# Third half of a fused attention and gated FFN: its q and k transposed by transfers instead of TensorE

## The chip, the cores and the metric

The kernel runs on one core of a Trainium2 chip. The metric is the device time of one execution in microseconds (us): the median of three runs is 237.72 us (236.86 to 237.77). The profiled execution took 237.94 us, of which the profile's span covers 236.1 us, at the full TensorE clock.

## The reference

Windowed attention with a linear distance bias, followed by a gated feed-forward layer over the same tokens (4 batches of 768 tokens, 8 heads of 64, feed-forward width 1536):

```python
scores = scale * q @ k.T                      # per batch and head, 768 x 768
keep   = (pos_k < 8) | ((rel >= 0) & (rel < 96))
scores = where(keep, scores - slope[h] * dist, -1e9)
a      = softmax(scores)
x      = (a @ v) -> [3072, 512]
out    = (relu(x @ w_gate) * (x @ w_val)) @ w_out
```

## The kernel before, in words

**Halves.** The 3072 tokens are cut into eight "halves" of 384, two to a batch, numbered 0 to 7. A half first goes through attention and then, as a chunk of 384 rows, through the feed-forward layer. The instruction order of every engine is written out by hand: `weave` takes a list of feed-forward pieces and drops other pieces at given fractions of it. `attention_pieces(s)` is the attention of half s, so TensorE does feed-forward products of earlier halves while it does the attention of the next.

**Operands of the scores.** TensorE needs q and k with the head dimension on the partitions, that is, transposed, and in bf16. `load_qk(s)` brings q and k of a half as float32 into `qs` and `ks`, which have one buffer each. Three routes lead on from there:

- Halves 0 and 1 use TensorE transposes with a layout of their own (`qTb`).
- Half 2, the third one, is cast by GpSimd into space of the result buffer `obuf` (`cast`, L263), eight casts in all, then transposed by TensorE against `ident` (`piece_t`, L299, into PSUM tiles of the pool `qk_ps`). VectorE moves the keys from PSUM into `kT[1]`, three copies for each pair of heads (`piece_copy_k`, L278 to L280), and ScalarE moves the queries into `qT2[0]` (L982). These are the four `T2_piece`s, placed at 0.55 to 0.95 of a weave of feed-forward products.
- Halves 3 to 7 use `early_pieces(s)`: GpSimd casts k and q into `kc` and `qc` (L367), transposing DMA transfers on the SP queue write `kN` and `qT2` (`piece_x`, L372, three for k and three for q), and GpSimd puts the keys in their order in `kT` (`piece_order`, L278 to L284).

**Values.** `load_v_half(s)` starts the loads of v on GpSimd's DMA queue. For an even half that is `load_v_globals` (L141, the first eight keys of the batch, which all queries see) and then four key tiles (L154); for batch 1 (half 2) three more tiles follow at once with `load_v_half(3)`. `spread_v_globals` (L146) copies the eight global rows into the six other key tiles by small DMA copies on the SP queue. The products of probabilities and values (L431) of half 2 need the first four key tiles and the first three of these copies.

**Weights.** `load_w_group(i)` loads 512 columns of `w_gate` and `w_val` each, cast to bf16 by the DMA; `wo_sb` is `w_out` as fp16. All are issued from GpSimd, so their data travel in the software DMA queue, in the order of issue, together with v and (for half 2 only) q and k. VectorE forms sums of blocks of `wo_sb` (L597) in the second weave, the first of them at 51.1 us.

**The order around the change.** On GpSimd: weight groups 1 and 2, q and k of half 2, `wo_sb`, some clearing of buffers, the eight casts, the loads of v. On the SP queue: nothing between the first loads of half 0 and the copies of global rows. On TensorE: the weave of feed-forward products of chunks 0 and 1 (L745), then from 48.3 us the scores of half 2 (L512), woven with the third weight group.

Of the kernel before, what the change touches and what calls it, by code (L numbers as in the profile page):

```python
# [16 lines left out]
def kernel(  # L17
# [12 lines left out]
    nc = tc.nc  # L30

    B, H, S, D = q.shape
# [6 lines left out]
    HP = H // 2  # L39
# [15 lines left out]
    for half in range(2):  # L55
# [35 lines left out]
    qT2 = [qTb[1].rearrange("d p e t -> d (p e t)")[:, i * HP * QH : (i + 1) * HP * QH].rearrange(  # L91
        "d (p t) -> d p t", p=HP) for i in range(2)]
# [20 lines left out]
    def load_qk(s, h0, h1, eng=nc.sync):  # L113
        b, half = divmod(s, 2)
        if s not in qs_of:
            qs_of[s] = stage.tile([128, H, NN * D], FP32, name="qs")
            ks_of[s] = stage.tile([128, H, NN * D], FP32, name="ks")
        for src, dst in ((k, ks_of[s]), (q, qs_of[s])):
            eng.dma_start(
                out=dst[:, h0:h1, :],  # L120
                in_=src[b, h0:h1, half * QH : (half + 1) * QH, :].rearrange(
                    "h (p n) d -> p h (n d)", n=NN))
# [17 lines left out]
    def load_v_globals(b):  # L140
        nc.gpsimd.dma_start(out=v_dst(b, 0, NG, 0),  # L141
                            in_=v[b, :, 0:NG, :].rearrange("h p d -> p h d"))

    def spread_v_globals(b, j0=1, j1=NT):
        for j in range(j0, j1):
            nc.sync.dma_start(out=v_dst(b, 0, NG, j), in_=v_dst(b, 0, NG, 0))  # L146
# [5 lines left out]
    def load_v(b, j, r0=0, r1=KT):  # L152
        n = min(r1, S - KT * j) - r0
        nc.gpsimd.dma_start(  # L154
            out=v_dst(b, NG + r0, NG + r0 + n, j),
            in_=v[b, :, KT * j + r0 : KT * j + r0 + n, :].rearrange("h p d -> p h d"))

    def fill_ones(eng, i, j):
        eng.memset(vbuf[i][:, j, :].bitcast(mybir.dt.uint32).rearrange(
            "p (h z) -> p h z", z=D // 2)[:, 0 : 2 * H + 1 : 2, :], 0x3F803F80)  # L160

    def load_v_half(s):
        b, half = divmod(s, 2)
        if half == 0:
            load_v_globals(b)
            spread_v_globals(b)
        for j in range(4) if half == 0 else range(4, NT):
            load_v(b, j)

    def load_w(dst, src, f0, f1):  # L170
        nc.gpsimd.dma_start(out=dst, in_=src[:, f0:f1].rearrange("(c p) f -> p c f", p=128))  # L171

    def load_w_group(i):
        load_w(wg[i], moe_w_gate, i * GW * 128, (i + 1) * GW * 128)
        load_w(wv[i], moe_w_val, i * GW * 128, (i + 1) * GW * 128)
# [67 lines left out]
    def setup_mask(h):  # L243
        nc.scalar.activation(m_all[:, h], dd, AF.Exp, bias=0.0, scale=-slopes[h])
# [6 lines left out]
    QKB, FFB, AVB = (qk_psum, "qk_ps"), (ff_psum, "ff_ps"), (av_psum, "av_ps")  # L251
# [6 lines left out]
    def piece_cast(s, p, i, eng):  # L258
        if (s, p) not in cast_of:
            cast_of[s, p] = oflat[:, 384 * p : 384 * (p + 1)].bitcast(BF16).rearrange(  # L260
                "t (i n e d) -> t i n e d", i=2, n=NN, e=2)
        src = (qs_of[s], ks_of[s])[i]
        (eng.copy if eng is nc.scalar else eng.tensor_copy)(  # L263
            cast_of[s, p][:, i].rearrange("t n e d -> t e n d"),
            src[:, 2 * p : 2 * p + 2, :].rearrange("t e (n d) -> t e n d", n=NN))

    def put_keys(copy, copy_small, kt, src, half):

        tk = src.rearrange("d (n p) -> d p n", n=NN)

        def put(j0, j1, p0, r0, r1):
            o = kt[:, j0:j1, r0:r1].rearrange("d j (p n) -> d j p n", n=NN)
            np_ = (r1 - r0) // NN
            i_ = tk[:, p0 : p0 + (j1 - j0) * np_, :].rearrange("d (j p) n -> d j p n", j=j1 - j0)
            return o, i_

        if half == 0:
            copy(*put(0, 3, 0, NG, 128))  # L278
            copy_small(*put(3, 4, 120, NG, NG + 24))
            copy_small(kt[:, :, 0:NG], kt[:, 0:1, NG : 2 * NG].to_broadcast([128, NT, NG]))  # L280
        else:
            copy(*put(4, 6, 32, NG, 128))
            copy_small(*put(3, 4, 0, NG + 24, 128))
            copy_small(*put(6, 7, 112, NG, NG + 48))  # L284

    tp_of = {}

    def piece_t(s, p, pool=av_psum, name="av_ps", apart=False):
        for i in (1, 0):
            if i == 1 or apart:  # L290
                tp = pool.tile([128, 512], FP32, name=name)
                tp = tp[:, 0:QH].bitcast(BF16).rearrange("d (i t) -> d i t", i=2)
            tp_of[s, p, i] = tp[:, i, :]
            for n in range(NN):
                for e in range(2 if s == 1 else 1):
                    r = slice(64 * e, 64 * e + 64) if s == 1 else slice(0, 128)
                    src = (qk16[s, i][:, 2 * p + e, n * D : (n + 1) * D] if s == 1
                           else cast_of[s, p][:, i, n])
                    nc.tensor.matmul(tp[r, i, n * 128 : (n + 1) * 128],  # L299
                                     lhsT=src, rhs=ident, is_transpose=True,  # L300
                                     start=((i == 1 or apart) and n == 0),
                                     stop=((i == 0 or apart) and n == NN - 1))

    def piece_copy_k(s, p):
        b, half = divmod(s, 2)
        put_keys(nc.vector.tensor_copy, nc.vector.tensor_copy, kT[b % 2][p], tp_of[s, p, 1], half)
# [59 lines left out]
    def piece_cast2(s, p, dst, src):  # L366
        nc.gpsimd.tensor_copy(  # L367
            dst[s % 2].rearrange("t n (h d) -> t h n d", d=D)[:, 2 * p : 2 * p + 2],
            src[s][:, 2 * p : 2 * p + 2, :].rearrange("t e (n d) -> t e n d", n=NN))

    def piece_x(dst, src, n):
        nc.sync.dma_start_transpose(out=dst[:, :, n * 128 : (n + 1) * 128], in_=src[:, n])  # L372

    def piece_order(s, p):
        b, half = divmod(s, 2)
        put_keys(nc.gpsimd.tensor_copy, nc.gpsimd.tensor_copy, kT[b % 2][p], kNb[s % 2][:, p], half)

    def early_pieces(s):
        out = [(0.0, lambda p=p: piece_cast2(s, p, kc, ks_of)) for p in range(HP)]
        out += [(0.0, lambda n=n: piece_x(kNb[s % 2], kc[s % 2], n)) for n in range(NN)]  # L380
        out += [(0.0, lambda p=p: piece_cast2(s, p, qc, qs_of)) for p in range(HP)]
        out += [(0.0, lambda n=n: piece_x(qT2[s % 2], qc[s % 2], n)) for n in range(NN)]
        out += [(0.0, lambda p=p: piece_order(s, p)) for p in range(HP)]
        return out
# [420 lines left out]
    def spread(items, first, last):  # L805

        n = len(items)
        return [(first + (i + 0.5) / n * (last - first), f) for i, (_, f) in enumerate(items)]

    def weave(f_items, *placed):  # L810
        total = sum(t for t, _ in f_items)
        a_items = sorted((x for p in placed for x in p), key=lambda x: x[0])
        done, ai = 0.0, 0
        for t, f in f_items:
            f()
            done += t
            while ai < len(a_items) and a_items[ai][0] * total <= done:
                a_items[ai][1]()
                ai += 1
        for _, f in a_items[ai:]:  # L820
            f()

    def cast(s, p, ek, eq):
        piece_cast(s, p, 1, ek)
        piece_cast(s, p, 0, eq)

    V, P, A = nc.vector, nc.gpsimd, nc.scalar
# [90 lines left out]
    piece_biased(1, 0)  # L918
    load_v(0, 3, 24)
    load_w_group(1)  # L920
    load_w_group(2)
    load_qk(2, 0, H, nc.gpsimd)
    load_w(wo_sb, moe_w_out, 0, DM)
    for f in gate[0:3]:
        f(0, LAST)
# [46 lines left out]
    nc.gpsimd.memset(vbuf[1][:, NT - 1, :].bitcast(mybir.dt.uint32), 0)  # L972
    for j in range(NT):
        fill_ones(nc.gpsimd, 1, j)
    for p in range(HP):
        cast(2, p, P, P)
    load_v_half(2)

    def T2_piece(p):
        piece_t(2, p, *QKB, apart=True)  # L980
        piece_copy_k(2, p)
        nc.scalar.copy(qT2[0][:, p], tp_of[2, p, 0])  # L982

    T2 = [(0.0, lambda p=p: T2_piece(p)) for p in range(HP)]
    weave(f1_1[G[0]] + f1_0[G[1]][4:] + f1_1[G[1]],
          [(0.05 + 0.06 * j, lambda j=j: fill_ones(nc.vector, 0, j)) for j in range(NT)],
          [(0.1 + 0.2 * i, lambda h=h: setup_mask(h)) for i, h in enumerate((0, 1, 6, 7))],
          [(0.6, lambda: load_qk(3, 0, H)), (0.6, lambda: load_v_half(3))],
          spread(T2, 0.55, 0.95))
    sums_wo = [(0.0, f) for i in (0, 3) for f in weight_sums(i, i + 3)]  # L990
    weave(f1_0[G[2]] + f1_1[G[2]] + f2_0 + f2_1,
          spread(attention_pieces(2), 0.02, 0.86), spread(early_pieces(3), 0.1, 0.76),
# [47 lines left out]
```

The softmax here doesn't subtract the row's maximum and nothing guards it: scores larger than these inputs give would overflow.

## Time and profile before

| what | value |
|---|---|
| median of three runs | 237.72 us |
| span of the profile | 236.1 us |
| TensorE busy | 228.7 us, 97% |
| VectorE busy | 186.9 us, 79% |
| ScalarE busy | 146.2 us, 62% |
| GpSimd busy | 89.0 us, 38% |
| mean DMA rate | 129 GB/s; in the four slices of 5.9 us from 23.6 to 47.2 us: 206, 262, 282, 171 |
| first load of weight group 1 to last landing of `wo_sb` | issued at 19.57 us, landed at 47.1 us |

Busy time of an engine is the union of its instructions. A DMA has two times: when the engine has issued it, and when it has landed; the DMA view gives the median from the one to the other. The DMA engines are sixteen and are shared by all queues: `q0` is the software queue fed by GpSimd, `q1` the hardware queue fed by SP. Their "share of 16 engines" counts the time of each packet from its start to its end; since packets overlap within an engine, a queue that keeps all engines full shows more than 100%.

### The profile page before, as it was taken

What the parts mean: (1) busy time and instruction counts of PE and PEld (TensorE: products, weight loads), DVE (VectorE), ACT (ScalarE), POOL (GpSimd) and SP (SyncE); (2) the same over time, 40 slices, a digit from 0 to 9 for tenths busy, and PEclk for the clock granted to TensorE, in tenths of its full rate; (3) what the DMA queues carried; (4) which work ended last, traced back from release to release, by engine and by line L of the source; (5) the groups of instructions that cost most, each with busy time, mean ns of one, the idle gap of its engine ahead of it and who ended that gap; (6) DMA issues with size and microseconds to landing.
All of it is one profiled execution on the core that took longest, in us unless ns stands there. A gap on an engine that the chain in (4) does not pass through costs nothing.

```text
span 236.1 us, 5512 instructions
## 1 busy us (share of the span) xinstructions
PE 228.7 (97%) x2021; PEld 157.7 (67%) x2021; DVE 186.9 (79%) x466; ACT 146.2 (62%) x321; POOL 89.0 (38%) x191
## 2 busy tenths in 40 slices
PE   7898999999999999999999999999999999999994
PEld 3674766656678666856688566856688566865683
DVE  6876867879988779886999779876899779863784
ACT  7988865667624887467842787557742687624310
POOL 8997913933483066406580066405340000000000
PEclk9999999999999999999999999999999999999999
DMA  5999999998459856856397764846412200020005
GB/s 167 203 168 183 206 262 282 171 118 267 72 155 170 250 149 106 52 176 204 90 81 119 236 175 90 53 143 214 93 44 89 92 0 3 0 92 0 1 3 178
DMA packets 71419, 30.43 MB, mean 129 GB/s; under 512 B 47744, under 2 KB 70784, under 8 KB 71392
## 3 DMA queue, kind: packets, MB, share of 16 engines
q0 software_dynamic: 34896, 10.27, 38.7%
q1 hardware_dynamic: 36496, 19.82, 29.7%
q8 instruction: 16, 0.26, 0.5%
q14 instruction: 11, 0.09, 0.1%
HBM read 28.38 MB, written 6.29 MB: 147 GB/s over the span
## 4 chain that ended last, share of the span: by engine, by line
PE 83%; DVE 5%; POOL 4%; DMA 4%; ACT 2%; issue 1%; POOLq 0%; DVEq 0%
PE ff_ps L745 49%; PE ff_ps L631 19%; PE av_ps L431 6%; DMA kc<-in_q_dram 4%; PE ff_ps L778 2%; PE av_ps L512 2%; PE qk_ps L512 2%; POOL vbuf L154 1%; DVE wo_sum L597 1%; DVE obuf L644 1%; DVE ht L761 1%; DVE es L533 1%; POOL kc L131 1%; PE av_ps L465 1%; POOL wg L171 1%
## 5 line engine op out<-in xcount | busy, mean ns | idle before, releaser
L754 ACT ACTIVATE grelu<-ff_ps 128x384 bf16<-128x384 f32 x96 | 46.8, 489 | 52.6 <-PE ff_ps L745 39.3
L745 PE MATMUL ff_ps<-xT,wg 128*128 128x384 bf16 x384 | 77.9, 326 | 0.2 <-DMA wg<-in_moe_w_gate_dram 0.2
L745 PE MATMUL ff_ps<-xT,wv 128*128 128x384 bf16 x384 | 77.9, 326 | 0.0
L761 DVE TENSOR_TENSOR ht<-ff_ps,grelu 128x384 f16<-128x384 f32 x96 | 53.4, 557 | 27.6 <-PE ff_ps L745 23.5
L745 PEld LDWEIGHTS <-wv 128*128 128x128 bf16 x384 | 36.0, 98 | 23.9 <-issue 1.1
L745 PEld LDWEIGHTS <-wg 128*128 128x128 bf16 x384 | 36.3, 97 | 21.7 <-issue 0.7
L450 DVE TENSOR_TENSOR xT<-av_ps,rcp 64x384 bf16<-64x384 f32 x48 | 26.6, 553 | 6.1 <-ACT rcp L445 5.3
L367 POOL CAST kc<-ks 128x384 bf16<-128x384 f32 x20 | 10.6, 569 | 54.5 <-DMA ks<-in_k_dram 54.5
L644 DVE TENSOR_TENSOR obuf<-ff_ps,obuf 128x512 f32<-128x512 f32 (+1 forms) x46 | 27.6, 604 | 3.6 <-PE ff_ps L631 0.9
L440 ACT ACTIVATE lnd<-av_ps 64x384 f32<-64x384 f32 x48 | 23.3, 485 | 11.1 <-PE av_ps L431 10.2
L533 DVE TENSOR_TENSOR es<-es,m_all 128x432 bf16<-128x432 bf16 (+3 forms) x108 | 29.9, 321 | 0.2 <-ACT es L521 0.2
L521 ACT ACTIVATE es<-qk_ps 128x432 bf16<-128x432 f32 (+2 forms) x54 | 27.6, 531 | 0.0
L154 POOL DMA_DIRECT2D vbuf<-in_v_dram x29 | 24.7, 860 | 0.1
L431 PEld LDWEIGHTS <-vbuf 128*128 128x128 bf16 x216 | 18.2, 98 | 4.8 <-DVE xT L450 0.4
L431 PE MATMUL av_ps<-es,vbuf 128*128 128x216 bf16 (+4 forms) x216 | 21.4, 226 | 0.0
L631 PEld LDWEIGHTS <-ht 128*128 128x128 f16 x198 | 18.6, 97 | 3.5 <-issue 0.8
L631 PEld LDWEIGHTS <-hsum 128*128 128x128 f16 x192 | 18.5, 98 | 2.1
L631 PE MATMUL ff_ps<-wo_sb,ht 128*128 128x256 f16 x132 | 18.3, 272 | 0.0
L631 PE MATMUL ff_ps<-wo_sum,hsum 128*128 128x256 f16 x144 | 17.2, 272 | 0.0
L445 ACT ACTIVATE rcp<-lnd 128x384 f32<-128x384 f32 x24 | 12.6, 523 | 0.8
L521 ACT ACTIVATE es<-av_ps 128x432 bf16<-128x432 f32 (+2 forms) x18 | 9.5, 527 | 2.0 <-PE qk_ps L512 2.0
L512 PEld LDWEIGHTS <-kT 64*128 64x128 bf16 x216 | 6.6, 94 | 6.1 <-issue 3.8
(130 smaller groups left out, 263.6 us busy)
## 6 DMA issues: line engine op xcount, KB each, us to landing
out_dram<-obuf SPq DMA_DIRECT2D x22, 256.0 KB
ks<-in_k_dram SPq DMA_DIRECT2D x5, 768.0 KB
qs<-in_q_dram SPq DMA_DIRECT2D x5, 768.0 KB
vbuf<-in_v_dram POOLq DMA_DIRECT2D x23, 120.0 KB, 4.7
wv<-in_moe_w_val_dram POOLq DMA_DIRECT2D x3, 512.0 KB, 10.5
wo_sb<-in_moe_w_out_dram POOLq DMA_DIRECT2D x1, 1536.0 KB, 21.0
wg<-in_moe_w_gate_dram POOLq DMA_DIRECT2D x2, 512.0 KB, 10.3
ks<-in_k_dram SPq DMA_DIRECT2D x4, 192.0 KB
```

Of the source, the lines that this page charges most:

```text
L154: nc.gpsimd.dma_start(out=v_dst(b, NG + r0, NG + r0 + n, j), in_=v[b, :, KT * j + r0 : KT * j + r0 + n, :].rearrange("h p d -> p h d"))
L431: nc.tensor.matmul(av3[:, :, a : a + w], lhsT=vb[:, j, z0 : z0 + 128], rhs=es[:, c : c + NN * w].rearrange("k (n p) -> k n p", n=NN), star ...
L440: nc.scalar.activation(ln[o0 : o0 + 64], av[d0 : d0 + 64, 0:QH], AF.Ln, bias=0.0, scale=1.0)
L450: nc.vector.tensor_tensor(xT_of[s][r, p, :], av_of[s, p, e][r, 0:QH], av_of[s, p, "r"][r], op=ALU.mult)
L512: nc.tensor.matmul(banks[e][:, c : c + NN * w], lhsT=kT[b % 2][p][r, j, :], rhs=q3[:, :, a : a + w], start=True, stop=True)
L521: nc.scalar.activation(es[:, 0:cols], ps[:, 0:cols], AF.Exp, bias=0.0, scale=scale)
L533: nc.vector.tensor_mul(e4, e4, mk)
L631: nc.tensor.matmul(ps[:, c0 : c0 + DH], lhsT=lhs(i), rhs=rhs(i), start=(i == 0), stop=(i == NP - 1), skip_group_check=True)
L644: add = lambda o, x, y: nc.vector.tensor_tensor(o, x, y, op=ALU.add)
L745: nc.tensor.matmul(st[key][:, 0:QH], lhsT=w_of(w, dc, fc), rhs=xT_of[c][:, dc, :], start=(dc == 0), stop=(dc == N_DC - 1))
L754: nc.scalar.activation(gr, psg[:, 0:QH], AF.Relu, bias=0.0, scale=1.0)
L761: nc.vector.tensor_tensor(ht[:, fc, :], psv[:, 0:QH], st["r", fc], op=ALU.mult)
```

## The change

Half 2 joins halves 3 to 7. The eight casts into `obuf`, the 24 TensorE transposes, the 12 copies by VectorE and the 4 by ScalarE go. In their place stand the pieces of `early_pieces(2)`, all issued one after the other where the casts stood: eight casts by GpSimd into `kc[0]` and `qc[0]`, six transposing transfers on the SP queue, and twelve copies by GpSimd that put the keys into `kT[1]`, ahead of the loads of v. To have q and k earlier, their loads are issued ahead of the third weight group. The purpose is to free TensorE, VectorE and ScalarE of the work.

```diff
     load_v(0, 3, 24)
     load_w_group(1)
+    load_qk(2, 0, H, nc.gpsimd)
     load_w_group(2)
-    load_qk(2, 0, H, nc.gpsimd)
     load_w(wo_sb, moe_w_out, 0, DM)
...
     for j in range(NT):
         fill_ones(nc.gpsimd, 1, j)
-    for p in range(HP):
-        cast(2, p, P, P)
+    for _, f in early_pieces(2):
+        f()
     load_v_half(2)
 
-    def T2_piece(p):
-        piece_t(2, p, *QKB, apart=True)
-        piece_copy_k(2, p)
-        nc.scalar.copy(qT2[0][:, p], tp_of[2, p, 0])
-
-    T2 = [(0.0, lambda p=p: T2_piece(p)) for p in range(HP)]
     weave(f1_1[G[0]] + f1_0[G[1]][4:] + f1_1[G[1]],
           [(0.05 + 0.06 * j, lambda j=j: fill_ones(nc.vector, 0, j)) for j in range(NT)],
           [(0.1 + 0.2 * i, lambda h=h: setup_mask(h)) for i, h in enumerate((0, 1, 6, 7))],
-          [(0.6, lambda: load_qk(3, 0, H)), (0.6, lambda: load_v_half(3))],
-          spread(T2, 0.55, 0.95))
+          [(0.6, lambda: load_qk(3, 0, H)), (0.6, lambda: load_v_half(3))])
```

## The prediction

> **What bounds the kernel now.** I read the page's busy times and its chain of waits first: TensorE is busy 97% of the span, and 83% of the chain that ended last is TensorE.
>
> ```profile
> PE 228.7 (97%) x2021; PEld 157.7 (67%) x2021; DVE 186.9 (79%) x466; ACT 146.2 (62%) x321; POOL 89.0 (38%) x191
> ...
> PE 83%; DVE 5%; POOL 4%; DMA 4%; ACT 2%; issue 1%; POOLq 0%; DVEq 0%
> ```
>
> Then TensorE's timeline where the four transposing pieces lie (start, length, line, tile, count).
>
> ```profile
> 39.72 0.81 PE L745 MATMUL ff_ps<-xT,wv 128*128 128x384 bf16 x4
> 40.37 0.50 PE L299 MATMUL qk_ps<-ident,obuf 128*128 128x128 bf16 x6
> 40.71 0.81 PE L745 MATMUL ff_ps<-xT,wg 128*128 128x384 bf16 x4
> ...
> 47.56 0.81 PE L745 MATMUL ff_ps<-xT,wv 128*128 128x384 bf16 x4
> 48.31 0.26 PE L512 MATMUL av_ps<-qT,kT 64*128 64x216 bf16 x1
> ```
>
> The starts count, not the modelled lengths: four products advance TensorE by 0.65 us (39.72 to 40.37), six transposes by 0.34 us (40.37 to 40.71), and no gap follows. What is taken off TensorE here shortens the path. At 48.31 us it starts the scores of half 2, which need all transposed queries and the keys of heads 0 to 3; at 54.57 us the value products, which need v.
>
> Last the GpSimd and SP timelines and the DMA view: which transfers fill the engines meanwhile?
>
> ```profile
> 37.70 0.50 POOL L263 CAST obuf<-ks 128x384 bf16<-128x384 f32 x1 [7.48 <-DMA ks<-in_k_dram]
> ...
> 42.83 0.62 POOL L141 DMA_DIRECT2D vbuf<-in_v_dram  x1
> ```
>
> ```profile
> 47.36 4.82 SPq L146 DMA_DIRECT2D vbuf<-vbuf  x6
> ...
> 59.65 3.92 SPq L372 DMA_TRANSPOSE kN<-kc  x3
> ```
>
> From 40 to 44 us the software queue alone holds all engines (packets, MB, share):
>
> ```profile
> q0 software_dynamic: 812, 0.83, 124.3%
> ```
>
> These are the 1,024-byte packets of `wo_sb`: 812 in 4 us, 203 in a us, so 79 ns of an engine each. The window from 20 to 32 us shows 148%, also full. The old route used no transfer here beyond the loads; the new one puts six into this stretch.
>
> **What the Trainium skill says.** "DMA: Bandwidth & Descriptors", section "Issuing engines are not separate DMA queues": transfers issued by any engine run on the same 16 DMA engines and interleave. The trace agrees: v alone ran 2,057 packets in 1.8 us (47.2 to 49.0), but beside output stores (73.7 to 74.2) only 129 in 0.5 us, 258 a us instead of 1,143. The same page, "Queues, rings and completion order": an engine goes round-robin between queues packet by packet, and its packet may hold several descriptors. The trace has one such meeting:
>
> ```profile
> q1 hardware_dynamic: 65, 0.13, 77.0%
> q0 software_dynamic: 129, 0.02, 50.2%
> ```
>
> Two of the one to one of the other: neither queue starves, but the grain of sharing (one record, or a whole transfer) isn't settled, least of all with 1,024-byte records against transposing ones. "GPSIMD Engine Reference", section 1, Specifications: GpSimd's SBUF interfaces are shared with VectorE. The trace shows little of it: GpSimd's casts take 0.51 us at 40 us beside a busy VectorE.
>
> **The change, part by part.**
>
> 1. *TensorE.* 24 transposes go, 4 x 0.335 = **1.34 us**, all on the path. The scores come due at 48.31 - 1.34 = 46.97 us, the values at 53.23 us.
> 2. *VectorE and ScalarE.* Twelve copies (4 x (0.52 + 0.17 + 0.32) = 4.0 us) and four (4 x 0.48 = 1.9 us) go. VectorE waits for TensorE's products between them (0.47 us before 43.95, 0.27 before 45.55), so they gain nothing. VectorE is full only from 50.4 to 59.3 us (8.88 of 8.90 us), and that stretch keeps its work.
> 3. *Earlier loads.* The second `wv` lands at 20.33 + 10.2 = 30.5 us; k landed 37.6 - 35.7 = 1.95 us after the third `wv`, so k now lands at 32.5, q at 34.5 us (37.6 and 39.6 before). The third weight group lands at 37 and 39.6 us instead of 33.2 and 35.7; its first use is at 48.8 us: nothing. `wo_sb` keeps its place.
> 4. *Casts.* Same number, same 0.45 us apart: k done at 34.5 us, q at 36.4. Hidden.
> 5. *Transposing transfers.* At 59.65 us, with idle engines, three took 3.9 us to issue, first packets came 1.3 us after the first issue, and the keys' copies started at 65.73, 6.1 us after (5.1 us after at 85.81 us). Unhindered: k from 34.5 to about 40, q issued from 38.4 to 42.2, landed at 44 us, 3 us ahead of the scores. But engines are full of weights until `wo_sb` is done. In all it is 6 x 512 = 3,072 packets of 256 bytes, 192 to an engine; at full burst they ran 1,080 a us (trace, 63.7 to 64.0 us), so 15 ns each, **2.8 us** of every engine, which something in the queue must wait.
> 6. *Key order.* Twelve GpSimd copies, 3.5 us as at 90.89 us, once the keys landed. Behind them on GpSimd wait the loads of v, and behind those the copies of global rows on SP, which TensorE's value products await.
> 7. *`wo_sb`.* It landed at 47.1 us; VectorE reads it first at 51.1, now 49.8 us. 47.1 + 2.8 = 49.9: at the edge, no more than 0.1 us.
>
> For the interleaving I take one for one: an engine that has both does one weight record (79 ns) and one transpose record (15 ns), 94 ns for the pair. The bounds are the transfers' own pace (they yield nothing) and starvation (they wait for long packets of the weights). From 35.8 us (34.5 + 1.3) the weights have until about 45.4 us of work left, 9.6 us or 121 records an engine. 96 pairs for k take 9.0 us: 44.8, landed a us later at 45.8; the keys of heads 0 to 3 are ready 1.8 us on, 47.6 us, all at 49.3. The other 25 pairs end the weights at 47.2 us; 71 query records are left, 15 to 40 ns each (burst, or SP's pace of 1.26 us for 32): 48.3 to 50.0, landed 49.3 to 51.0, middle **50.2 us**. TensorE stands still from 46.97 to 50.2 us: 3.2 lost, 1.34 gained, **+1.9 us**. Values: issue at 49.3, global rows landed 2 us later, three copies (0.8 us each to issue, 3 us to land, as before: issued up to 49.7, landed 52.7) at 56.7 us, against 54.57 + 1.9 = 56.5: no more than 0.2 us on top. So 237.7 + 1.9 = **239.6 us**.
>
> **The rivals.**
>
> - *A, hidden.* The transfers fit into gaps and delay nothing: 237.72 - 1.34 = **236.4 us**. For: 3 us of slack, and the later halves run this route unseen. Against: no gap is seen before 45 us, and engine time adds up.
> - *B, own pace.* The transfers go through unhindered (for: at 73.7 us the stores kept 130 packets a us against 141 alone, and v yielded). Then q is there at 44 to 46 us, but 2.8 us of engine time push back `wo_sb`, the global rows behind it, and the copies: 52.7 + 2.8 = 55.5 us against 54.57 to 54.77 before: +0.8, **238.5 us**, 238 to 239.
> - *D, starved.* The hardware queue gets a turn only after long packets of weights, so nearly all transposing waits until 45.4 us: k landed at 48, keys ordered at 51.5, global rows at 53.5, copies at 58 us: +3.4, **241.2 us**, up to 242.
>
> **How the numbers follow.** One for one (forecast C) 0.36, B 0.24, A 0.22, D 0.18. Faster by over 0.5% (below 236.5 us) is A and a little of B: 0.24. Within 0.5% (to 238.9 us) is most of B and the lower edge of C: 0.24. Slower: 0.52. The range reaches from A at 236.3 to the middle of D, 241.7 us.
>
> **What would show it.** Right: the gap between the last products and the first scores of half 2 grows to some 3 us, with transposing DMA as its releaser; the SP queue's L372 at 34.5 us has packets still running at 46 us; loads of v issued near 49 us rather than 42.8. B: no gap at the scores, but one of 1 to 2 us before the first L431. A: no gap at either. Wrong altogether: a TensorE gap at the first `wg` of the third group (landed after 48 us), or GpSimd's twelve copies far above 3.5 us beside VectorE.

## The result, and the profile after

The changed kernel takes 246.31 us, median of six runs (245.92 to 247.39), against 237.68 us for the kernel before (six runs). The ratio is 1.038 (95% interval 1.035 to 1.041): 8.6 us slower, where 1.9 had been forecast. The profiled span grew from 236.1 to 244.7 us.

The page of the kernel after: busy time and chain of waits, to be laid beside the two lines of before.

```profile
PE 231.0 (94%) x1997; PEld 157.4 (64%) x1997; DVE 185.0 (76%) x454; ACT 144.5 (59%) x317; POOL 92.0 (38%) x203
...
PE 68%; DMA 17%; POOL 8%; DVE 2%; ACT 1%; SPq 1%; issue 1%; POOLq 0%; DVEq 0%
```

TensorE has 24 instructions fewer, yet its busy time rose by 2.3 us: some of its work ran slower. In the chain TensorE fell from 83% to 68%, and transfers rose from 4% to 17%.

TensorE's timeline of after, from the last products ahead of half 2's scores to the first value products. The bracket is the idle time ahead of an instruction and what ended it.

```profile
46.17 0.81 PE L745 MATMUL ff_ps<-xT,wv 128*128 128x384 bf16 x4
51.32 0.25 PE L512 MATMUL av_ps<-qT,kT 64*128 64x216 bf16 x1 [4.34 <-POOL kT L278]
...
52.17 1.46 PE L745 MATMUL ff_ps<-xT,wg 128*128 128x384 bf16 x4
53.43 1.49 PE L745 MATMUL ff_ps<-xT,wv 128*128 128x384 bf16 x4
...
56.27 0.81 PE L745 MATMUL ff_ps<-xT,wg 128*128 128x384 bf16 x4
...
59.45 0.35 PE L431 MATMUL av_ps<-es,vbuf 128*128 128x216 bf16 x2
60.82 0.24 PE L431 MATMUL av_ps<-es,vbuf 128*128 128x144 bf16 x1 [1.02 <-DMA vbuf<-in_v_dram]
61.81 0.19 PE L431 MATMUL av_ps<-es,vbuf 128*128 128x24 bf16 x1 [0.75 <-DMA vbuf<-in_v_dram]
61.85 1.26 PE L745 MATMUL ff_ps<-xT,wg 128*128 128x384 bf16 x4
```

Compare starts with before:

| TensorE reaches | before | after | behind |
|---|---|---|---|
| first scores of half 2 (L512) | 48.31 | 51.32 | 3.0 |
| the fifth group of four products after them | 51.40 | 56.27 | 4.9 |
| first value products (L431) | 54.57 | 59.45 | 4.9 |
| the products after these | 54.85 | 61.85 | 7.0 |
| next scores (L512) | 59.33 | 67.78 | 8.5 |

Two of these steps are waits: 4.3 us at the scores (less the 1.3 gained by the missing transposes), and 1.8 us at the value products, for v (1.02 and 0.75 in the brackets; the whole step is 2.1). The other two steps have no wait in them: the four products at 52.17 us take 1.26 us to the next ones where 0.65 was usual. The windows of the trace name the reason; columns are the stretch, its length, TensorE's busy time and instructions, the granted clock (the share of its full speed that TensorE was given), the DMA share and GB/s.

```profile
51.50:52.00 0.50, 0.44 (x8) 0.83 0.00 0
52.00:54.00 2.00, 2.00 (x10) 0.50 0.00 0
55.00:55.50 0.50, 0.50 (x4) 0.76 0.34 46
...
62.00:62.50 0.50, 0.50 (x3) 0.57 1.97 139
62.50:64.00 1.50, 1.50 (x6) 0.50 1.14 267
65.00:65.50 0.50, 0.50 (x3) 0.52 1.02 336
65.50:66.00 0.50, 0.50 (x5) 1.00 1.07 358
```

After each wait TensorE's clock is half of full speed, twice, each time for some 3.4 us of work. In the kernel before it is 1.00 through this stretch. That is about 1.7 to 1.9 us each time.

Why the keys were so late stands on GpSimd's and SP's timelines of after: first SP's six transposing transfers, then GpSimd's first keys' copy and the loads of v.

```profile
34.50 4.23 SPq L372 DMA_TRANSPOSE kN<-kc  x3
38.89 8.33 SPq L372 DMA_TRANSPOSE qT<-qc  x3
```

```profile
49.95 0.53 POOL L278 COPY kT<-kN 128x360 bf16<-128x360 bf16 x1 [13.54 <-DMA kN<-kc]
...
53.64 0.62 POOL L141 DMA_DIRECT2D vbuf<-in_v_dram  x1 [0.31 <-issue]
54.25 6.04 POOL L154 DMA_DIRECT2D vbuf<-in_v_dram  x7
```

The first transposing transfer was issued at 34.50 us, just when it was forecast. The keys' copies start 15.5 us after that, where at idle engines the later halves need 5 to 6 us; GpSimd waits 13.5 us for them. Two windows of the DMA view tell where the time went. From 34.5 to 38 us one queue only appears:

```profile
q0 software_dynamic: 727, 0.72, 124.1%
```

and from 39 to 45 us two:

```profile
q0 software_dynamic: 923, 0.94, 92.1%
q1 hardware_dynamic: 926, 0.23, 29.6%
```

For 3.9 us after its issue the transposing transfer got nothing; from then on as many of its 256-byte records went as 1,024-byte records of the weights, 926 to 923 in 6 us. `wo_sb` landed at 49.7 us, 2.6 later than before.

So the 8.6 us are read thus: v is there at 61.8 us instead of in time, which puts the products behind the first value products 7.0 us back, whatever TensorE did until then; and the slow clock after that wait costs another 1.7 us. The experiments test both halves.

### The profile page after: what moved, and what is told of

The parts are those of the page before. It is cut to its first block, busy times and chain, and to the rows that moved or that the text cites. A ratio compares the mean times of both kernels' runs of the same rounds, so it can differ in the third digit from the quotient of the medians.

```text
span 244.7 us, 5458 instructions
## 1 busy us (share of the span) xinstructions
PE 231.0 (94%) x1997; PEld 157.4 (64%) x1997; DVE 185.0 (76%) x454; ACT 144.5 (59%) x317; POOL 92.0 (38%) x203
## 4 chain that ended last, share of the span: by engine, by line
PE 68%; DMA 17%; POOL 8%; DVE 2%; ACT 1%; SPq 1%; issue 1%; POOLq 0%; DVEq 0%
PE ff_ps L745 41%; PE ff_ps L631 17%; PE av_ps L431 5%; DMA kN<-kc 5%; DMA ks<-in_k_dram 5%; DMA wv<-in_moe_w_val_dram 3%; POOL vbuf L154 2%; DMA vbuf<-in_v_dram 2%; PE av_ps L512 2%; DVE obuf L644 2%; DMA out_dram<-obuf 2%; PE qk_ps L512 1%; POOL kc L131 1%; PE ff_ps L778 1%; SPq L372 1%
## 5 line engine op out<-in xcount | busy, mean ns | idle before, releaser
L754 ACT ACTIVATE grelu<-ff_ps 128x384 bf16<-128x384 f32 x96 | 46.8, 490 | 57.5 <-PE ff_ps L745 42.5
L745 PE MATMUL ff_ps<-xT,wg 128*128 128x384 bf16 x384 | 79.6, 331 | 0.4 <-DMA wg<-in_moe_w_gate_dram 0.4
L745 PE MATMUL ff_ps<-xT,wv 128*128 128x384 bf16 x384 | 79.3, 330 | 0.1
L745 PEld LDWEIGHTS <-wg 128*128 128x128 bf16 x384 | 37.0, 99 | 23.6 <-issue 2.4
L533 DVE TENSOR_TENSOR es<-es,m_all 128x432 bf16<-128x432 bf16 (+3 forms) x108 | 30.8, 330 | 4.9 <-ACT es L521 4.9
L367 POOL CAST kc<-ks 128x384 bf16<-128x384 f32 x24 | 11.9, 538 | 55.4 <-DMA ks<-in_k_dram 55.4
L431 PE MATMUL av_ps<-es,vbuf 128*128 128x216 bf16 (+4 forms) x216 | 22.0, 228 | 1.8 <-DMA vbuf<-in_v_dram 1.8
L431 PEld LDWEIGHTS <-vbuf 128*128 128x128 bf16 x216 | 18.6, 99 | 6.9 <-DMA vbuf<-in_v_dram 2.2
L278 POOL COPY kT<-kN 128x360 bf16<-128x360 bf16 x12 | 7.0, 587 | 19.4 <-DMA kN<-kc 19.4
L512 PEld LDWEIGHTS <-kT 64*128 64x128 bf16 x216 | 6.6, 94 | 10.6 <-POOL kT L278 4.7
```

The costliest lines, as they stand in the source:

```text
L431: nc.tensor.matmul(av3[:, :, a : a + w], lhsT=vb[:, j, z0 : z0 + 128], rhs=es[:, c : c + NN * w].rearrange("k (n p) -> k n p", n=NN), star ...
L512: nc.tensor.matmul(banks[e][:, c : c + NN * w], lhsT=kT[b % 2][p][r, j, :], rhs=q3[:, :, a : a + w], start=True, stop=True)
L533: nc.vector.tensor_mul(e4, e4, mk)
L745: nc.tensor.matmul(st[key][:, 0:QH], lhsT=w_of(w, dc, fc), rhs=xT_of[c][:, dc, :], start=(dc == 0), stop=(dc == N_DC - 1))
L754: nc.scalar.activation(gr, psg[:, 0:QH], AF.Relu, bias=0.0, scale=1.0)
```

## The experiments

Each was timed beside the kernel before on the same chip; ratios are to that.

### The earlier loads alone

The kernel before with the first hunk of the diff and nothing else.

```diff
+    load_qk(2, 0, H, nc.gpsimd)
     load_w_group(2)
-    load_qk(2, 0, H, nc.gpsimd)
```

> The kernel before with only the order of loads changed: q and k of the third half ahead of the third weight group, TensorE route kept. Theory (the loads' order is harmless, the cost is in the transposing transfers): q and k land some 5 us earlier (32.5 and 34.5 us), GpSimd casts earlier, the third weight group lands by 40 us and is due at 48.8: 237.7 us, no change. Rival (the later weight group is what costs): TensorE gap at its first product, several us slower.

Measured: 237.71 us over 12 runs, ratio 0.9995 (0.9973 to 1.0017). In its trace TensorE waits for nothing from 30 to 60 us. The order of the loads is harmless; the loss lies in the route.

### Values ahead of the keys' copies, without and with work for TensorE in the gap

If v is late because its loads stand behind the keys' copies on GpSimd, move them ahead. The second kernel also gives TensorE twenty products of zeros ahead of the scores, to keep its clock.

```diff
-    for _, f in early_pieces(2):
-        f()
-    load_v_half(2)
+    early2 = [f for _, f in early_pieces(2)]
+    for f in early2[:-HP]:
+        f()
+    load_v_half(2)
+    for f in early2[-HP:]:      # the keys' copies
+        f()
...
+    warm_up(20)                 # second kernel only
     sums_wo = [(0.0, f) for i in (0, 3) for f in weight_sums(i, i + 3)]
```

> The changed kernel with the loads of v issued right after the eight casts, ahead of GpSimd's twelve copies of keys. Theory (the keys landing late hold GpSimd, which holds the loads of v; that second wait and the slow TensorE clock after it are 2.1 + 1.7 us of the loss): scores still start at 51.3 us, no wait at the first value products, 246.3 - 3.8 = 242.5 us. Rival (v is late because the engines are full, whatever the time of issue): the wait at the value products stays at about 2 us, 246 us.

> As the run with v first, and 20 products on zeros (128x512 each, 0.21 us, results unused) on TensorE ahead of the third half's scores, to fill its wait. Theory (after an idle wait TensorE's clock is held down for some 3 us, which costs 1.9 us): products after the scores take 0.65 us for four at once, not 1.27; 242.5 - 1.9 = 240.6 us. Rival (the slow products wait for PSUM buffers or for ScalarE and VectorE catching up): fillers change nothing, 242.5 us.

Measured: 248.18 us (ratio 1.043, 1.036 to 1.049) and 246.82 us (1.037, 1.030 to 1.045). Both expectations missed. The wait for v did go, but TensorE's timeline of the first kernel shows what took its place:

```profile
56.27 0.34 PE L512 MATMUL av_ps<-qT,kT 64*128 64x216 bf16 x1 [9.07 <-DMA qT<-qc]
```

The keys landed at 50.7 us, much as in the changed kernel; the queries at 56.1 instead of 51.2. Now v's transfers run where the queries' do, and the queries take the loss. Moving v alone exchanges one late transfer for another.

The clock in this kernel, from the windows of its trace:

```profile
48.00:50.00 2.00, 0.00 (x0) 1.00 1.71 111
50.00:52.00 2.00, 0.00 (x0) 0.67 1.98 83
52.00:54.00 2.00, 0.00 (x0) 0.50 1.79 139
...
58.00:60.00 2.00, 2.00 (x8) 0.50 1.23 193
60.00:62.00 2.00, 2.00 (x11) 0.77 1.06 338
```

It falls while TensorE still stands idle, so the clock answers to idleness, not to a late buffer. In the profiled execution of the kernel with zeros TensorE had waited only 3.3 us and worked on at full speed, four products in 0.67 us. The zeros don't ensure it: in the other three executions of that kernel the mean clock was 0.984 to 0.993.

```profile
54.81 0.25 PE L512 MATMUL av_ps<-qT,kT 64*128 64x216 bf16 x1 [3.29 <-DMA qT<-qc]
...
55.28 0.82 PE L745 MATMUL ff_ps<-xT,wg 128*128 128x384 bf16 x4
55.95 0.81 PE L745 MATMUL ff_ps<-xT,wv 128*128 128x384 bf16 x4
```

### Zeros in the gaps of the changed kernel

The changed kernel with twenty products of zeros ahead of the scores and eighteen ahead of the first value products; and with the first of the two alone.

```diff
+    warm_up(20)
     sums_wo = [(0.0, f) for i in (0, 3) for f in weight_sums(i, i + 3)]
...
-AV = lambda p: [(0.0, lambda e=e: (flush(), piece_av(s, p, e))) for e in range(2)]
+AV = lambda p: [(0.0, lambda e=e: (flush(), (s, p, e) == (2, 0, 0) and warm_up(18), piece_av(s, p, e))) for e in range(2)]
```

> The changed kernel with 20 such products ahead of the scores and 18 ahead of the first value products. Theory: v lands at 61.8 us whatever TensorE does, so the first fill only lengthens the second wait; the second fill saves the slow clock after it, 1.7 us: 244.6 us. Rival (both slow stretches are lost time of their own, so both fills pay): 246.3 - 3.6 = 242.7 us. Rival (no clock effect): 246.3 us.

> The changed kernel with 20 zero products ahead of the scores alone. Theory: TensorE's clock stays up and it reaches the value products 1.9 us sooner, where v is not there before 61.8 us, so the wait grows by as much: 246.3 us, no gain, against 245.05 us with both fills. Rival (each slow stretch counts): 244.4 us.

Measured: 245.05 us with both (ratio 1.031, 1.024 to 1.038), mean clock 0.999 to 1.0; 246.34 us with the first alone (1.039, 1.033 to 1.045), no different from the changed kernel's 246.31. In the trace with the first alone TensorE reaches the value products at 57.30 us, 2.1 sooner than in the changed kernel, and then waits 2.75 us for v, which is in at 60.8 us there (GpSimd issued it 0.5 us sooner). So the first wait and its slow clock cost next to nothing in the end, because v holds TensorE at about 61 us anyhow. The median is no clean price of it: in two of the four executions the mean clock was 0.984 and 0.985, as low as in the changed kernel, and these took 246.90 and 247.42 us, the other two 245.23 and 245.78.

The slow clock behind the wait for v is paid: about 1.3 us by the medians, 1.7 by the ratios (whose intervals still overlap), 1.7 by the trace. What remains is the late v: with both fills the products behind the first value products start at 61.47 us, 6.6 behind before, right after the zeros end, and the fourth tile of v, issued at 56.5 us and landed 4.4 to 4.6 us later, had not been in much sooner.

### `wo_sb` out of the way, and the same for the TensorE route

The change's own mechanism, tested from the other side: v right after the casts, and the 1.5 MB of `wo_sb` issued only after the keys' copies, so that no long weight transfer runs beside the transposes. The sums that read `wo_sb` move to 0.3 to 0.56 of their weave. The control has the TensorE route of before with `wo_sb` equally late.

```diff
-    load_w(wo_sb, moe_w_out, 0, DM)
...
     for f in early2[-HP:]:
         f()
+    load_w(wo_sb, moe_w_out, 0, DM)
...
-          spread(sums_wo, 0.08, 0.4))
+          spread(sums_wo, 0.3, 0.56))
```

> The changed kernel with the loads of v issued right after the casts, wo_sb (1.5 MB) issued after GpSimd's copies of keys instead of ahead of them, and VectorE's block sums moved from 0.08-0.4 to 0.3-0.56 of the second weave. Theory (the transposing records go one for one with whatever record is queued on the software queue, so 79 ns weights slow them and 15 ns v records hardly do): packets start at 38.2 us as before, k landed at 43, q at 45.5 us, no wait at the scores (due 46.97) and none at the values; wo_sb lands at 56 us; 237.7 - 1.34 = 236.4 us. Rival (transposing transfers are slow of themselves in this stretch): q still lands at 51 us, 243 us or more.

> Control: the kernel before (TensorE route) with the same late wo_sb and late block sums. Both theories: 237.7 us if the late sums cost nothing; what it differs by is the price of the later wo_sb alone, to be taken off the run with wo_sb late.

Measured: 245.84 us (ratio 1.034, 1.028 to 1.040) and 245.54 us (1.034, 1.031 to 1.038). The time missed the expectation by 9 us, but the part in question came out as it should. TensorE's timeline of the first:

```profile
46.80 0.25 PE L512 MATMUL av_ps<-qT,kT 64*128 64x216 bf16 x1 [0.62 <-DMA qT<-qc]
...
63.14 0.36 PE L512 MATMUL av_ps<-qT,kT 64*128 64x216 bf16 x1 [5.47 <-DVE xT L450]
```

The scores start at 46.80 us, 1.5 ahead of before (0.9 of it were there ahead of the transposes, and 0.6 are lost again waiting for the last queries), and the value products at 53.06 without a wait. What is lost comes ten microseconds later, and is VectorE's wait ahead of the sums:

```profile
62.06 0.56 DVE L597 TENSOR_TENSOR wo_sum<-wo_sb 128x768 f16<-128x768 f16 x1 [6.31 <-DMA wo_sb<-in_moe_w_out_dram]
```

`wo_sb` was expected at 56 us and landed at 62.0. From 51 to 59 us the DMA view of this kernel has

```profile
q0 software_dynamic: 1030, 1.05, 77.4%
q1 hardware_dynamic: 1032, 0.78, 39.4%
```

that is, the next half's q and k, loaded by SP in 768-byte records, went one for one with the records of `wo_sb`. The same sharing that had delayed the transposes now delayed the weights. The control lands `wo_sb` at 62.3 us and waits alike, so these 8 us belong to the late `wo_sb`, not to the route.

### The third weight group out of the way too

As the kernel above, but with the third weight group also behind the casts. The software queue is then empty when the first transpose is issued.

```diff
-    load_w_group(2)
...
     for f in early2[:-HP]:
         f()
+    load_w_group(2)
     load_v_half(2)
```

> As the run with wo_sb late, and the third weight group also issued only after the casts, so that the software queue is empty when the first transposing transfer is issued at 34.5 us. Theory (its first packets wait for weight records already queued: 2.6 us more than the 1.3 us of an idle stretch): first packets at 35.8 instead of 38.4 us, k landed by 40.5 us; q shares with the third group and lands at 46 to 47 us; 236.4 to 237 us. Rival (the start is late for another reason, SP or GpSimd): first packets at 38.4 us again.

Measured: 249.83 us (ratio 1.052, 1.045 to 1.059): the time missed, the start did not. The time is lost in two waits of TensorE: 3.9 us at the scores, for queries that came at 50.7 us instead of 46 to 47, and 3.0 us later on, behind sums that waited for `wo_sb` until 65.2 us. The first transpose was issued at 33.98 us. The DMA view from 35 to 36 us, and then from 38 to 41.5 us:

```profile
q1 hardware_dynamic: 532, 0.13, 57.8%
```

```profile
q0 software_dynamic: 508, 0.51, 107.0%
q1 hardware_dynamic: 33, 0.00, 1.3%
```

With nothing queued ahead, records flow 1.0 us after the issue, 532 in a us. The third transposing transfer of the keys, issued by 37.9 us behind the weight group, got next to nothing for some 4 us and landed at 46.4. So a transfer seems to wait behind one that is already queued, and only then to share record for record; the 508 weight records that passed it are about one transfer of the group (512 KB). From 46 to 48 us, where both queues hold small records (v's 128 bytes, the transposes' 256), they are again even:

```profile
q1 hardware_dynamic: 855, 0.20, 81.2%
q0 software_dynamic: 860, 0.10, 81.0%
```

### Fourth half's loads behind `wo_sb`, for both routes

To let `wo_sb` land sooner, the fourth half's q and k go to the software queue behind it, in the transposing kernel and in its TensorE control.

```diff
-          [(0.6, lambda: load_qk(3, 0, H)), (0.6, lambda: load_v_half(3))])
+          [(0.6, lambda: load_qk(3, 0, H, nc.gpsimd)), (0.6, lambda: load_v_half(3))])
...
-          spread(sums_wo, 0.3, 0.56))
+          spread(sums_wo, 0.36, 0.57))
```

> The run with wo_sb late, with q and k of the fourth half loaded from GpSimd behind wo_sb instead of from SP beside it, and VectorE's block sums at 0.36-0.57 of the second weave. Theory (what cost 8 us there was wo_sb landing at 62 us, since those loads took every other record): wo_sb lands at 56.5 us, ahead of the first sum at 57.5; no TensorE wait is left, the clock stays up, and the 1.34 us of TensorE transposes show at last: 236.4 us. Rival (the late sums crowd VectorE, or transposing beside v has a cost of its own): 238 us or more.

> Control: the TensorE route with the same late wo_sb, loads of the fourth half from GpSimd and late sums. Theory: 237.7 us, so that the other run is 1.34 us below it; if both lie higher by the same amount, that is the price of the late sums, and the difference is still 1.34 us. Rival: no difference between the two routes.

Measured: 242.78 us (ratio 1.022, 1.019 to 1.025) by transfers, 244.38 us (1.028, 1.025 to 1.031) by TensorE. The two differ by 1.6 us. The sharper reading is TensorE's timeline, first of the transposing kernel, then of the control:

```profile
46.24 0.26 PE L512 MATMUL av_ps<-qT,kT 64*128 64x216 bf16 x1
...
57.96 1.47 PE L778 MATMUL ff_ps<-wo_sb,ht 128*128 128x512 f16 x6 [0.40 <-ACT es L521]
...
67.04 0.80 PE L631 MATMUL ff_ps<-wo_sum,ht 128*128 128x256 f16 x3 [4.14 <-DVE wo_sum L597]
```

```profile
47.71 0.26 PE L512 MATMUL av_ps<-qT,kT 64*128 64x216 bf16 x1
...
59.48 1.47 PE L778 MATMUL ff_ps<-wo_sb,ht 128*128 128x512 f16 x6 [0.45 <-ACT es L521]
...
68.57 0.80 PE L631 MATMUL ff_ps<-wo_sum,ht 128*128 128x256 f16 x3 [4.14 <-DVE wo_sum L597]
```

The scores of half 2 start without a wait in both, and 1.47 us sooner in the first, before anything reads `wo_sb`. Ahead of the transposes it led by 0.13 us (the same product starts at 36.39 and 36.52 us), so the transposes' gain is 1.34 us, as forecast. That it lasts to the end is not owed to the transposes alone: VectorE's first sum waits for `wo_sb` in both (0.58 and 0.63 us), and `wo_sb`, issued 0.8 us sooner in the first, landed 1.5 us sooner. What both lose is in VectorE's sums, still too late.

### Sums earlier, and `wo_sb` sooner

The transposing kernel again, with `wo_sb` issued ahead of the last two keys' copies and the six sums needed first placed ahead of the other two: at 0.31 to 0.44 of the weave, and, in a second kernel, at 0.35 to 0.48.

```diff
+    g0, g1 = (list(weight_sums(i, i + 3)) for i in (0, 3))
+    sums_wo = [(0.0, f) for f in g0[0:3] + g1[0:3] + [g0[3], g1[3]]]
...
-          spread(sums_wo, 0.36, 0.57))
+          spread(sums_wo[0:6], 0.31, 0.44), spread(sums_wo[6:], 0.5, 0.57))
```

> The transfer route as in the run with late wo_sb and GpSimd's loads of the fourth half, with wo_sb issued 1.6 us sooner (after two of the four key orders), and VectorE's block sums in another order: the six that the next products need first, at 0.31-0.44 of the second weave, the last two at 0.5-0.57. Theory (all that was left to lose there was TensorE's 4.1 us wait for the sums and the slow clock after it, 2.8 us): wo_sb lands at 56.3 us, a wait of up to 1 us on VectorE, no idle TensorE: 236.4 to 237.5 us. Rival (the sums don't fit between wo_sb's landing and their use): a wait at the products of the sums remains, 239 us or more.

> The same with the six sums at 0.35-0.48 and the last two at 0.52-0.57. Theory: no wait of VectorE for wo_sb, six sums done by 62 us, when they are due: 236.4 to 237.5 us. Rival: GpSimd's casts from 58 us on lengthen VectorE's sums from 0.55 to 0.85 us as in that run, the sums end at 63.5 us, TensorE waits 1 us: 237.5 to 238.5 us.

Measured: 241.48 us (ratio 1.018, 1.014 to 1.021) and 239.75 us (1.013, 1.008 to 1.017). Both improve on 242.78, neither beats before: the rivals of both expectations, that TensorE still waits for sums, came true, by more than they said. Two of the six executions of the second took 242.2 and 242.8 us at a mean clock of 0.985, the others 239.3 to 239.9. In the second VectorE's sums and TensorE's wait for them read:

```profile
59.80 0.55 DVE L597 TENSOR_TENSOR wo_sum<-wo_sb,wo_sum 128x768 f16<-128x768 f16 x1
61.05 0.85 DVE L597 TENSOR_TENSOR wo_sum<-wo_sb 128x768 f16<-128x768 f16 x1
63.20 0.85 DVE L597 TENSOR_TENSOR wo_sum<-wo_sb,wo_sum 128x768 f16<-128x768 f16 x1
64.57 0.85 DVE L597 TENSOR_TENSOR wo_sum<-wo_sb,wo_sum 128x768 f16<-128x768 f16 x1
```

```profile
65.48 0.49 PE L631 MATMUL ff_ps<-wo_sum,ht 128*128 128x256 f16 x3 [2.04 <-DVE wo_sum L597]
```

The three sums of 0.85 us lie beside GpSimd's casts (59.35 to 65.0 us), which at the same time take 2.9 us for four instead of 1.86. The sum at 59.80 kept its 0.55 us; it started just ahead of a cast, and that cast took 0.91 us. `wo_sb` thus has no place in this kernel that is early enough for the sums and late enough for the transposes, of those that were tried.

## Why the prediction was wrong in size and right in direction

What it had right, step by step: 1.34 us of transposes on the path (the two routes with GpSimd's loads of the fourth half); k and q landing at 32.5 and 34.5 us and the first transpose issued at 34.50; the casts hidden; sharing one for one with the weights, once both queues ran; 2.8 us of engine time which `wo_sb` has to wait (2.6); queries landed at 51.2, just past the forecast 49.3 to 51.0; a wait at the scores that ends with transposing transfers; and v issued behind the keys' copies. The earlier loads cost nothing, as the first experiment shows. Rivals A (hidden) and B (own pace) fail on the wait at the scores. D (starved) came nearest in time, yet not in mechanism: the hardware queue was starved for its first 3.9 us only.

Four terms failed.

1. **The start (part 5).** Records were to flow from 35.8 us, 1.3 us after the issue, a delay read at idle engines. Behind a queued weight transfer it was 3.9 us: 2.6 us later. The empty queue with its 1.0 us bears out the reason.
2. **The pair.** 94 ns for one weight and one transposing record; 923 pairs in 6 us over 16 engines are 104 ns. Over 96 pairs that is 1 us. With the start, the keys landed at 49.8, not 45.8 us. Start and pair make 3.6 of these 4.0 us. So the scores waited for the keys rather than the queries, and lost 3.0, not 1.9 us. On this the Trainium skill, "DMA: Bandwidth & Descriptors", section "Queues, rings and completion order", speaks of whole packets of several descriptors in turn. The counts here show equal numbers of records once both queues run; how many make a turn they don't tell. The long wait at the start is measured here.
3. **Values (the last step of the sum).** It said no more than 0.2 us on top, by way of the copies of global rows. What was last were the tiles of v themselves. GpSimd needs 0.62 us for the global rows and then begins a tile every 0.92 us, and the fourth tile lands 4.8 us after its issue begins: 53.64 + 0.62 + 3 x 0.92 + 4.8 = 61.8 us, which is where TensorE's last wait for v ends. Worked out so with the forecast's own 49.3 us it gives 57.5 us, 1.0 us past the 56.5 when it was due, not 0.2. So this chain was mis-sized even before the keys came late; 4 us more of late keys did the rest. This is the step that failed most: at the products behind the first value products the forecast had 2.1 us of delay (1.9 and 0.2), the trace has 7.0.
4. **The clock, which is not in the sum at all.** The Trainium skill, "TensorE: Matmul & The Clock Gate", "Part 1: The HAM clock gate", gives half speed after an idle window of about 3.4 us that runs free of the work, and full speed after a busy one. The trace agrees on the length of the window. Taking the share of half speed in each stretch shown above, the clock falls at 51.83 us, rises at 55.24, falls at 62.07, rises at 65.48: steps of 3.41, 6.83 and 3.41 us. The kernel with v first has 50.68 to 60.92, three times 3.41. The trace does not agree that the whole window must be idle. TensorE was busy for 0.45 us in the window ahead of the first fall and for 1.64 us in that ahead of the second (columns as above; half speed follows each):

```profile
48.42:51.83 3.41, 0.45 (x6) 1.00 0.88 103
58.66:62.07 3.41, 1.64 (x12) 1.00 2.23 143
```

The forecast gap, 46.97 to 50.2 us, would have put 1.4 and 1.8 us of idling into two windows of this run, and whether that lowers the clock stays open (last section). But behind the values, where the sum had 0.2 us of waiting, 1.7 us fell due and nothing was charged.

Terms 1 to 3 make the products behind the first value products 7.0 us late, term 4 adds 1.7, which gives 8.7 us against 8.6 measured. The range stopped at D, which followed the late keys through GpSimd only to the copies of global rows, not to the tiles of v, and charged no slow clock.

## What to carry to other kernels

Work moved from a full engine to transfers isn't free when the transfer engines are full in that stretch: price it at the pace of the longest records that it shares with, plus the rest of what is queued ahead, and then follow the late landing through the in-order engine that waits for it, down to the landing of the last load issued behind it. If TensorE then stands idle for about half of a 3.4 us window or more, add half a window, 1.7 us, for the slower clock. A saving of 1.3 us on the bounding engine does not pay for such a chain. With `wo_sb` out of the way the transposes did gain it against their control, though no kernel tried here beat the one before.

## What of the hardware was not expected

- **Sharing by record, not by byte.** Two busy queues moved equal numbers of records: 923 to 926 of 1,024 and 256 bytes, 1,030 to 1,032 of 1,024 and 768 bytes, 860 to 855 of 128 and 256 bytes. The queue with the long records keeps most of the bandwidth, and a stream of short records is slowed to their pace. It is not so everywhere: the prediction's window beside the stores has 129 to 65, and the kernel with v first has 1,226 to 580 (128 and 256 bytes) from 52 to 54 us, with queries still outstanding.
- **A late start behind a queued transfer.** 3.9 us from issue to first records in the changed kernel, 1.0 us with an empty queue.
- **A partly busy window also lowers the clock.** In the window from 58.66 to 62.07 us of the changed kernel TensorE waited only 1.8 of 3.41 us, and the clock was halved all the same. Cut into such windows, the profiled executions show ten at full speed with 2.0 to 3.4 us of idling ahead of the last stores, and half speed followed all ten; 1.4 us or less never brought it. Between them it went both ways: after 1.77 us (this window) the clock fell, after 1.80, 1.82 and 1.92 us in three other kernels it did not. After these waits full speed came back only behind a window without idling; three slow windows with 0.8 to 1.0 us of it were followed by another slow one, 1.7 us more.
- **Two-input sums of VectorE beside GpSimd's casts.** The sums took 0.85 us instead of 0.55, four casts 2.9 instead of 1.86. "GPSIMD Engine Reference" of the Trainium skill, section 1, Specifications, has them share SBUF interfaces where VectorE reads two inputs; this is its size here. The prediction had seen little of it in casts beside other VectorE work.
